# Leftover rows of four batches as seven half-size products, input loads issued behind GpSimd's first sums of the second chunk, both normalisations behind the second transpose

## The chip, the cores and the metric

The kernel runs on one core of a Trainium2 chip. The metric is the device time of one execution in microseconds (us). Three runs of the kernel before took 236.84, 237.04 and 237.11 us; their median, 237.04 us, is the time before. Engine names are those of the profile: PE is the matrix engine and PEld its weight load, DVE the vector engine, ACT the scalar engine, POOL is GpSimd, SP the sync engine, which here only issues DMAs.

## The reference, cut to what matters

There are 8 batches, each with 8 heads, 576 rows and 64 columns a head; `phi` gives 32 memory slots a head. An attention over the memory slots is followed by a gated feed-forward block with d_model 512 and d_ff 1536.

```python
a = exp(phi - max(phi, axis=2)); a = a / (sum(a, axis=2) + 1e-09)     # over the 576 rows
k_m = einsum('bhsm,bhsd->bhmd', a, k); v_m = einsum('bhsm,bhsd->bhmd', a, v)
scores = q @ k_m.T / 8; attn = softmax(scores)                         # over the 32 slots
x = (attn @ v_m), heads side by side                                   # 4608 x 512
out = (silu(x @ w_gate) * (x @ w_val)) @ w_out
```

## The kernel before, in words

**Stages of a batch.** The order of all instructions is written out by hand; each engine runs its own list in program order. For a batch the kernel exponentiates `phi` on ACT (`phi_exp`, line 176), forms the memory keys and values on PE (`kv_sum`, line 235) with their denominators (`kv_denominators`, line 263), scales them on DVE (`kv_reciprocal`, `kv_norm`, lines 267 and 271), and transposes them (`kv_T`). For batches 4 and on, `kv_T` is a DMA on SP's queue. The value side is folded into the weights (`u_round`, line 471, copied out of PSUM by ACT and DVE, lines 491 and 495). Scores (line 400) are exponentiated on ACT (line 411), their sums come from a transposing DVE reduction (`z_inv_v`, lines 434 to 443), and `norm` (line 451) gives the weights `t_A`.

**Gate and value slots.** 24 slots a batch (`gv_slot`) each make one gate and one value product (two matmuls each, line 514); ACT takes the gate through silu (line 531) and DVE multiplies it with the value (line 537) into `t_h`. A slot runs its gate, then the value and the multiplication of the slot before it. Eight slots make one of three chunks of d_ff.

**The output product.** `t_h` times `w_out` is done for the first 512 rows of a batch by a Winograd form: 7 products instead of 8 of half the size, each 12 matmuls of 128x256 (`products`, line 706). The left-hand sums `t_S` are made when a chunk is done (`chunk_done`, lines 601 and 559): on POOL for chunks 0 and 1, on DVE for chunk 2, four operations a chunk. PSUM banks are named `p_os`, `p_oa` and `p_oc`. ACT keeps three intermediate results (`keep`, line 729: `t_p` twice and `t_q`), DVE adds (line 734). In batches 0 to 6 the order is: first (two products, on s and then a), five (on c), six (on s, kept as `t_q`), three (on c), seven (on s again, over the same bank that `t_q` was copied from), four (on s).

**Leftover rows.** 64 rows of each batch remain. They are copied by POOL into `xs` (line 591), two batches side by side, and `out_rest` (line 654) multiplies them plainly: 12 matmuls a half, 24 a pair of batches, 96 in all.

**One iteration of the main loop, for batch b = 3 to 6.** It starts with product one of batch b-1 (6 units of 2 matmuls), then `loads(b)`, which has POOL issue four DMAs for batch b+2, in the order q, phi, k, v; then `scores(b)`, `u_values`, product two of batch b-1, `z_inv_v`, `norm`, product five, `phi_exp(b+1)` on ACT, `z_inv_v` and `norm` for the second half, product six, products three and seven. Then come the 24 slots. `spread` lays other work among them: what is left of batch b-1's units (product four, then 6 units of `out_rest`), after the eighth slot `kv_items(b+1)` with one `u_item` and two units behind it, and around slot 19 `u_three(b+1)`. `load_qT(b+1)`, a transposing DMA on SP's queue, and `phi_sum(b+1)`, six POOL operations (lines 215 to 224) that make the denominators a matter of two matmuls, stand at the head of the slots. For b = 2 `loads(2)` stands at slot 7 and batch 3 has no `phi_sum`. Iteration 7 has neither loads nor a next batch.

**Double buffers.** `phi` and `k`/`v` have two buffers each, q one for even and one for odd batches.

Of the kernel before, what the change touches and what calls it, by code (L numbers as in the profile page):

```python
# [14 lines left out]
def kernel(  # L15
# [19 lines left out]
    nc = tc.nc  # L35
# [173 lines left out]
    def phi_sum(b):  # L209
# [4 lines left out]
        mark = att.tile([1, 1], BF16, tag="mark", bufs=1, name="t_mark")  # L214
        nc.gpsimd.tensor_copy(out=mark, in_=atts[b - 1, 1][0:1, 0, 0:1])  # L215
# [81 lines left out]
    def kv_items(b, beside=None):  # L297


        def run_sums():  # L300
            o = 2 * D
            p = [bank([128, CH], FP32, f"p_kv{g}") for g in range(NG)]
            kv_denominators(b, p[0][:, o:o + NG])
            kv_sum(b, p, (0, 1))
            kv_reciprocal(b, p[0][:, o:o + NG])
            kv_norm(b, p)
            done(*p)
            if beside:
                beside()

        return [run_sums, lambda: kv_T(b)]
# [273 lines left out]
    def chunk_done(b, c):  # L585
# [21 lines left out]
        end = c + 1 == NCH  # L607
        if (b, c) in ((0, 2), (1, 1), (1, 2)):
            late.append(lambda *part: sums(nc.gpsimd if b else nc.vector, *part))
        else:  # L610
            sums(nc.vector if end else nc.gpsimd)
        if end and b > 1:
            late.append(ends)
        else:
            ends()
        if (b, c) in beside_sums:
            beside_sums[b, c]()

# [4 lines left out]
    }  # L623

# [10 lines left out]
    def store(t_o, b, t0, count, row=0, cols=slice(0, 512), queues=None):  # L635
# [3 lines left out]
        for n, (r0, m, bb, jj, pp) in enumerate(token_segments(b, t0, count)):  # L639
            eng = queues[n % len(queues)] if queues else nc.sync  # L640
            eng.dma_start(out=out_r[bb, jj, pp:pp + m, cols], in_=t_o[row + r0:row + r0 + m])

    def out_rest(pair, half):

        h = DM // 2
        mine = {}
        cols = slice(h * half, h * half + h)

        def unit(n):
            def run():  # L650
                if n == 0:
                    mine["p"] = bank([128, h], FP32, "p_oo")
                for jf in (2 * n, 2 * n + 1):
                    nc.tensor.matmul(  # L654
                        mine["p"],
                        lhsT=xs[pair][:, jf].rearrange("p a t -> p (a t)"),
                        rhs=WO[jf][:, cols],
                        start=(jf == 0),
                        stop=(jf == NJF - 1),
                    )  # L660
                if n == NJF // 2 - 1:
                    t_o = work.tile([128, h], FP32, tag="to", name="t_o")
                    copy("v" if box.get("end") else "a", t_o, mine["p"])
                    done(mine["p"])
                    end = 2 * pair + 2 == B
                    for k in range(2):
                        store(
                            t_o, 2 * pair + k, S - 64, 64, 64 * k, cols,
                            ((nc.sync, nc.scalar)[k],) if end else None,
                        )  # L670

            return run

        return [unit(n) for n in range(NJF // 2)]

    def products(b, by_hand):
# [3 lines left out]
        lo, hi = slice(0, h), slice(h, DM)  # L680

        def A(e, n):
            return lambda c, m, u: hts[b, c][
# [3 lines left out]
        def Sx(n):  # L687
            return lambda c, m, u: Ss[b, c][:, n, m, 128 * u:128 * u + 128]
# [7 lines left out]
        def product(home, lhs, rhs, after):  # L696
            def unit(k):
                c, m = k // 2, k % 2

                def run():  # L700
                    fresh = k == 0 and home not in mine
                    if fresh:
                        mine[home] = bank([128, 2, h], FP32, f"p_o{home}")
                        mine[home, "new"] = True
                    for u in range(2):
# [21 lines left out]
        def keep(name, home):  # L727
            def run():
                nc.scalar.copy(out=tile_of(name, tag=name, bufs=1), in_=mine[home])
# [8 lines left out]
        def both(name, t0, cols):  # L738
            for u in range(2):
                store(mine[name][:, u, cols], b, t0 + 128 * u, 128, cols=cols)  # L740

        def c11():
            t = tile_of("o1", (128, 2, DM), tag="to")
            add(t[:, :, lo], "a", "p1", True)
            if box.get("end"):
                both("o1", 0, lo)

        def c22():
            t = tile_of("o2", (128, 2, DM), tag="to")
            add(t[:, :, hi], "s", "p5")  # L750
            if box.get("end"):
                both("o2", 256, hi)

        def c12():
            t = mine["o1"]
            add(t[:, :, hi], "c", "q6", True)
            both("o1", 0, hi if box.get("end") else slice(0, DM))

        def c21():
            t = mine["o2"]  # L760
            copy("v" if box.get("end") else "a", t[:, :, lo], mine["s"])
            done(mine["s"])
            both("o2", 256, lo if box.get("end") else slice(0, DM))
# [4 lines left out]
        )  # L768
        now = {n: f for n, f in ops.items() if n not in by_hand}
# [6 lines left out]
        if b + 1 == B:  # L776
# [177 lines left out]
    for b in range(2, B):  # L954
        last = b + 1 == B
        exp_tables()
        if b == 2:
# [15 lines left out]
            mark = att.tile([1, 1], BF16, tag="mark", bufs=1, name="t_mark")  # L973
            nc.gpsimd.tensor_copy(out=mark, in_=Ts[2][0:1, 3, 0, 0:1])
# [5 lines left out]
        else:  # L980
            backlog += out_rest(b // 2 - 1, b % 2)
            run(take(6))
        if b > 2:
            loads(b)
# [9 lines left out]
        norm(b, 0)  # L994
# [4 lines left out]
        z_inv_v(b, 1)  # L999
        norm(b, 1)  # L1000
        run(take(6))
        run_late()
        nc.scalar.preload_act_table_set("silu_and_others")
        run(take(12))
        if b == 2:
            u_three(2)
            run(out_rest(0, 0))
            u_values(2)
            backlog = one[36:]
        g = gv_slots(b)  # L1010
        beside = 0 if last else min(7, len(backlog))
        outs = [lambda: run(take(1)) for _ in range(len(backlog) - beside)]
        streams = [(g, 0, 24), (outs, 4, 24)]
        if last:
            streams += [([u_item(b, 2)], 5, 6)]
        if not last:
            load_qT(b + 1)
            if b > 2:
                phi_sum(b + 1)
            else:  # L1020
                streams += [([lambda: loads(2)], 7, 8)]
            streams += [
                (kv_items(b + 1, lambda: (u_item(b, 2, "aava")(), run(take(2)))), KV, KV + 4),
                ([lambda: (run(take(2)), u_three(b + 1), run(take(3)))], 19, 20),
# [8 lines left out]
    run(out_rest(B // 2 - 1, 0))  # L1033
# [4 lines left out]
    run(out_rest(B // 2 - 1, 1))  # L1038
# [28 lines left out]
```

The softmax here doesn't subtract the row's maximum and nothing guards it: scores larger than these inputs give would overflow.

## Time and profile before

| what | value |
|---|---|
| median of three runs | 237.04 us |
| the profiled execution's own time | 236.3 us |
| its span, first to last instruction | 234.5 us |
| PE busy | 225.9 us, 96% |
| DVE, ACT, POOL busy | 187.4, 172.5, 135.2 us |
| last matmul ends | 230.2 us |
| POOL starts chunk 0's sums in batches 2 to 6 | 84.36, 109.25, 134.49, 159.79, 185.09 us |
| POOL issues the phi load of batches 4 to 7 | 74.80, 95.45, 119.86, 145.10 us |
| ACT starts `phi_exp` of batches 4 to 7 | 98.45, 124.08, 149.31, 174.62 us |

All times within the execution count from the start of the span. The profiled execution took 236.3 us, 0.74 us less than the median; its span leaves out 1.8 us around it. In the timeline view a row has the start, the time from the first start to the last end of the merged instructions, the engine, the line of the kernel, the operation, what it writes and reads, how many instructions the row merges and, in brackets, the idle time before it and what ended it. For matmuls such a row ends about 0.16 us after the next one has started, since they are pipelined.

### The profile page before, as it was taken

How to read it: one execution, taken by the hardware profiler on the slowest of the kernel's cores; microseconds unless marked ns; L12 is line 12 of the kernel's file. 1: busy time of each engine (PE TensorE's matmuls, PEld its weight loads, DVE VectorE, ACT ScalarE, POOL GpSimd, SP SyncE). 2: the span in 40 equal slices, each digit the busy share in tenths (PEclk: the TensorE clock that was granted, in tenths of full speed). 3: DMA queues.
4: the chain of work that ended last, by engine and by line, in shares of the span. 5: the costliest groups of instructions: out<-in, count | busy, mean ns of one | idle time of the engine just before them, and what ended most of it. 6: DMA issues, size and time to landing. Idle time of an engine off the chain costs nothing.

```text
span 234.5 us, 7300 instructions
## 1 busy us (share of the span) xinstructions
PE 225.9 (96%) x2847; PEld 171.3 (73%) x2847; DVE 187.4 (80%) x417; ACT 172.5 (74%) x368; POOL 135.2 (58%) x171
## 2 busy tenths in 40 slices
PE   7998899999999999999999999999999999999992
PEld 2555466778887777887778777877788777878881
DVE  4157699999979697998799878988799879987621
ACT  2758888988447888977898779968897789677310
POOL 8532426999099159654992399267916493029400
PEclk9999999999999999999999999999999999999999
DMA  6999999999974999899559964999313721122134
GB/s 211 205 205 207 198 208 206 228 238 248 207 169 97 252 216 158 166 247 232 137 80 252 214 110 106 225 226 142 110 25 81 132 89 27 31 62 89 33 92 126
DMA packets 42914, 36.84 MB, mean 157 GB/s; under 512 B 15488, under 2 KB 38528, under 8 KB 42880
## 3 DMA queue, kind: packets, MB, share of 16 engines
q0 software_dynamic: 21440, 22.42, 55.0%
q1 hardware_dynamic: 20176, 12.79, 25.8%
q10 hardware_dynamic: 1264, 1.18, 1.6%
q8 instruction: 22, 0.36, 0.6%
q14 instruction: 12, 0.10, 0.1%
HBM read 42.47 MB, written 9.44 MB: 221 GB/s over the span
## 4 chain that ended last, share of the span: by engine, by line
PE 82%; DMA 8%; POOL 4%; DVE 3%; issue 1%; ACT 0%; DVEq 0%; POOLq 0%
PE p_g L514 20%; PE p_v L514 19%; PE p_os L706 16%; PE p_oc L706 8%; DMA t_kv<-in_v_dram 8%; PE p_u L471 5%; PE p_oo L654 5%; PE p_oa L706 4%; PE p_kv L235 2%; POOL t_es L217 1%; POOL t_q L108 1%; PE p_g L400 1%; POOL t_kv L98 1%; DVE t_lz L443 1%; DVE t_z L434 1%
## 5 line engine op out<-in xcount | busy, mean ns | idle before, releaser
L537 DVE TENSOR_TENSOR t_h<-t_sg,p_v 128x288 bf16<-128x288 bf16 x192 | 83.1, 452 | 15.6 <-PE p_v L514 7.6
L514 PEld LDWEIGHTS <-t_U 128*128 128x128 bf16 x768 | 73.7, 98 | 21.7 <-issue 2.9
L531 ACT ACTIVATE t_sg<-p_g 128x288 bf16<-128x288 f32 x192 | 74.5, 423 | 15.9 <-PE p_g L514 9.1
L514 PE MATMUL p_g<-t_A,t_U 128*128 128x288 bf16 x384 | 77.2, 286 | 0.0
L514 PE MATMUL p_v<-t_A,t_U 128*128 128x288 bf16 x384 | 77.0, 286 | 0.0
L706 PEld LDWEIGHTS <-t_S 128*128 128x128 bf16 x384 | 37.4, 98 | 4.5 <-issue 0.2
L601 POOL TENSOR_TENSOR t_S<-t_h 128x512 bf16<-128x512 bf16 x17 | 19.7, 1156 | 35.2 <-DVE t_h L537 35.2
L491 ACT CAST t_U<-p_u 128x512 bf16<-128x512 f32 x53 | 28.0, 608 | 8.9 <-PE p_u L471 8.9
L706 PEld LDWEIGHTS <-t_h 128*128 128x128 bf16 x288 | 27.3, 98 | 7.8 <-issue 4.0
L706 PE MATMUL p_os<-t_T,t_S 128*128 128x256 bf16 x192 | 23.7, 273 | 0.0
L559 POOL TENSOR_TENSOR t_S<-t_S,t_h 128x512 bf16<-128x512 bf16 x17 | 19.6, 1155 | 1.3
L559 POOL TENSOR_TENSOR t_S<-t_h,t_S 128x512 bf16<-128x512 bf16 x17 | 20.1, 1186 | 0.0
L559 POOL TENSOR_TENSOR t_S<-t_h 128x512 bf16<-128x512 bf16 x17 | 19.6, 1155 | 0.0
L471 PE MATMUL p_u<-W,t_kT 64*32 64x512 bf16 (+1 forms) x416 | 15.9, 363 | 0.1
L706 PE MATMUL p_os<-t_T,t_h 128*128 128x256 bf16 x96 | 15.6, 273 | 0.0
L827 PE MATMUL p_warm<-bones 128*128 128x512 bf16 (+2 forms) x43 | 12.9, 427 | 1.7 <-DVE bones L850 1.7
L451 DVE TENSOR_TENSOR t_A<-t_E,t_lz 128x576 bf16<-128x576 bf16 x16 | 13.4, 840 | 0.9 <-ACT t_lz L427 0.3
L654 PE MATMUL p_oo<-WO,t_x 128*128 128x256 bf16 x96 | 14.0, 273 | 0.0
L495 DVE CAST t_U<-p_u 128x512 bf16<-128x512 f32 x19 | 12.4, 683 | 1.6 <-PE p_u L471 1.6
L215 POOL COPY t_mark<-t_A 1x1 bf16<-1x1 bf16 x4 | 0.7, 182 | 20.3 <-DVE t_A L451 20.3
L706 PE MATMUL p_oc<-t_T,t_S 128*128 128x256 bf16 x96 | 12.0, 273 | 0.0
L706 PE MATMUL p_oa<-WO,t_h 128*128 128x256 bf16 x96 | 11.8, 273 | 0.0
(93 smaller groups left out, 309.9 us busy)
## 6 DMA issues: line engine op xcount, KB each, us to landing
t_kv<-in_k_dram POOLq DMA_DIRECT2D x8, 576.0 KB, 10.1
t_kv<-in_v_dram POOLq DMA_DIRECT2D x8, 576.0 KB, 14.4
out_dram<-t_o SPq DMA_DIRECT2D x21, 192.0 KB, 2.6
t_phi<-in_phi_dram POOLq DMA_DIRECT2D x6, 576.0 KB, 7.9
t_q<-in_q_dram POOLq DMA_DIRECT2D x5, 576.0 KB, 7.4
out_dram<-t_o SPq DMA_DIRECT2D x37, 64.0 KB, 2.0
out_dram<-t_o SPq DMA_DIRECT2D x14, 128.0 KB, 5.8
t_q<-in_q_dram POOLq DMA_DIRECT2D x6, 288.0 KB, 11.3
```

What stands on the lines that cost most here:

```text
L451: nc.vector.tensor_tensor(out=a, in0=es.pop((b, g)), in1=lzs.pop((b, g)), op=ALU.mult)
L471: nc.tensor.matmul(p[g][32 * i:32 * i + 32, o:o + n], lhsT=kTs[b][64 * g:64 * g + 64, 2, 32 * i:32 * i + 32], rhs=w_part(w, c, i, g, halve ...
L491: nc.scalar.copy(out=t, in_=p)
L495: nc.vector.tensor_copy(out=t, in_=p)
L514: nc.tensor.matmul(p[:, 0:HALF], lhsT=Us[b, c, g][:, o // 2, which, 128 * (o % 2):128 * (o % 2 + 1)], rhs=atts[b, g][:, r], start=(g == 0) ...
L531: nc.scalar.activation(out=sg, in_=gate[:, 0:HALF], func=AF.Silu)
L537: nc.vector.tensor_tensor(out=dst, in0=sg, in1=val[:, 0:HALF], op=ALU.mult)
L559: eng.tensor_tensor(out=out, in0=x, in1=y, op=ALU.subtract)
L601: eng.tensor_tensor(out=t[:, 0], in0=A21, in1=A22, op=ALU.add)
L654: nc.tensor.matmul(mine["p"], lhsT=xs[pair][:, jf].rearrange("p a t -> p (a t)"), rhs=WO[jf][:, cols], start=(jf == 0), stop=(jf == NJF - 1),)
L706: nc.tensor.matmul(mine[home][:, u], lhsT=lhs(c, m, u), rhs=rhs(c, m), start=fresh and u == 0, stop=(k == 5), skip_group_check=u == 1 or n ...
L827: nc.tensor.matmul(p[:, 0:128 * a], lhsT=bones, rhs=x.to_broadcast([128, a, 128]) if a > 1 else bones, start=True, stop=True,)
```

## The change

Six things change.

1. The leftovers of four batches (two `xs` tiles of 128 rows) are one 256-row block, done as seven Winograd products of half the rows: 6 matmuls a product, 42 for four batches in place of 48. `out_rest` is gone. The left-hand sums come from `quad_sums`: 12 operations on 128x256 elements, on POOL for batches 0 to 3; for batches 4 to 7 nine on POOL and three on DVE. The first block stands in iteration 4, 12 units in slots 0 to 3 and 30 in slots 12 to 18.5; the second has 12 units in iteration 7's slots and 30 at the end.
2. `loads(b)`, for all b from 2, moves from the head of iteration b (slot 7 for b = 2) into `chunk_done(b, 1)`: POOL issues the four DMAs after the first two sums of chunk 1 and a copy.
3. From batch 2 on POOL's other two sums of chunk 1 come behind chunk 2's sums on DVE; POOL waits for these with a one-element copy (`wait_for`).
4. In `kv_items` of batches 4, 6 and 7 the denominators, and with them the reciprocal and the scaling on DVE, come behind the sums, the `u_item` and its two units. For batch 5 there is no `phi_sum`; its denominators are nine matmuls ahead of the sums, as for batch 3 before.
5. Both `norm` calls stand behind the second `z_inv_v`.
6. Product four of the batch before is spread thinner: 2 units in slots 3 to 24, two behind `u_item`, two behind `u_three`; in iteration 4 all six in slots 3 to 7. Stores alternate between queues at the end.

```diff
@@ phi_sum, new wait_for @@
-        mark = att.tile([1, 1], BF16, tag="mark", bufs=1, name="t_mark")
-        nc.gpsimd.tensor_copy(out=mark, in_=atts[b - 1, 1][0:1, 0, 0:1])
+        wait_for(atts[b - 1, 1][0:1, 0, 0:1])
...
+    def wait_for(x):
+        t = att.tile([1, 1], BF16, tag="mark", bufs=1, name="t_mark")
+        nc.gpsimd.tensor_copy(out=t, in_=x)
@@ kv_items @@
-            kv_denominators(b, p[0][:, o:o + NG])
+            behind = b in esums
+            if not behind:
+                kv_denominators(b, p[0][:, o:o + NG])
             kv_sum(b, p, (0, 1))
+            if behind:
+                beside()
+                kv_denominators(b, p[0][:, o:o + NG])
             kv_reciprocal(b, p[0][:, o:o + NG])
             kv_norm(b, p)
             done(*p)
-            if beside:
+            if beside and not behind:
                 beside()
@@ chunk_done @@
+        fourth = b in (3, 7)
         if (b, c) in ((0, 2), (1, 1), (1, 2)):
             late.append(lambda *part: sums(nc.gpsimd if b else nc.vector, *part))
+        elif b < 2:
+            sums(nc.gpsimd)
+        elif end:
+            sums(nc.vector)
+            wait_for(t[0:1, 3, 0, 0:1])
+            for part in ((2,), (3,)) if b + 1 == B else ((3,), (2,)):
+                for f in second:
+                    f(nc.gpsimd, part)
+            second.clear()
         else:
-            sums(nc.vector if end else nc.gpsimd)
-        if end and b > 1:
+            if c:
+                sums(nc.gpsimd, (0, 1))
+                second.append(sums)
+            else:
+                sums(nc.gpsimd)
+        if end and b > 1 and not fourth:
             late.append(ends)
         else:
             ends()
+        if b > 1 and c == 1:
+            loads(b)
+        if b + 1 == B and end:
+            quad_sums(1, (0, 1, 2))
@@ quad_sums, new @@
+        for n in parts:
+            for c in range(NCH):
+                t = Qs[qd, c]
+                A11, A12, A21, A22 = quarters(c)
+                if n == 0:
+                    nc.gpsimd.tensor_tensor(out=t[:, 0], in0=A21, in1=A22, op=ALU.add)
+                elif n == 1:
+                    subtract(nc.gpsimd, t[:, 1], t[:, 0], A11)
+                elif n == 2:
+                    subtract(nc.gpsimd, A21, A11, A21)
+                else:
+                    subtract(nc.vector if qd else nc.gpsimd, t[:, 2], A12, t[:, 1])
@@ products(b, by_hand, quad=None) @@
+        U = 2 if quad is None else 1
...
-                    for u in range(2):
+                    for u in range(U):
...
+        if quad is not None:
+            ops.update(
+                c11=leftover("c11", None, 0, lo), c12=leftover("c12", "q6", 1, hi),
+                c22=leftover("c22", "p5", 1, hi), c21=leftover("c21", "q6", 0, lo),
+            )
-        if b + 1 == B:
+        if quad is not None or b + 1 == B:
             return first + six + five + seven + three + four, ops
@@ main loop @@
         else:
-            backlog += out_rest(b // 2 - 1, b % 2)
             run(take(6))
-        if b > 2:
-            loads(b)
...
         z_inv_v(b, 0)
-        norm(b, 0)
         ops["c11"]()
         run(take(6))
         if not last:
             phi_exp(b + 1)
         z_inv_v(b, 1)
+        norm(b, 0)
         norm(b, 1)
         run(take(6))
         run_late()
+        if b == 4:
+            wait_for(atts[4, 1][0:1, 0, 0:1])
+            quad_sums(0)
...
         if b == 2:
             u_three(2)
-            run(out_rest(0, 0))
+            run(one[36:])
             u_values(2)
-            backlog = one[36:]
         g = gv_slots(b)
-        beside = 0 if last else min(7, len(backlog))
+        quad = []
+        if b == 4:
+            quad = products(b, (), 0)[0]
+        if last:
+            rest, rest_ops = products(b, (), 1)
+            backlog += rest[:12]
+        beside = 0 if last or quad else min(4, len(backlog))
         outs = [lambda: run(take(1)) for _ in range(len(backlog) - beside)]
-        streams = [(g, 0, 24), (outs, 4, 24)]
+        streams = [(g, 0, 24), (quad[:12], 0, 3), (quad[12:], 12, 18.5)]
+        streams += [(outs, 3, 7 if quad else 24)]
...
-            if b > 2:
+            if b > 2 and b != 4:
                 phi_sum(b + 1)
-            else:
-                streams += [([lambda: loads(2)], 7, 8)]
             streams += [
                 (kv_items(b + 1, lambda: (u_item(b, 2, "aava")(), run(take(2)))), KV, KV + 4),
-                ([lambda: (run(take(2)), u_three(b + 1), run(take(3)))], 19, 20),
+                ([lambda: (u_three(b + 1), run(take(2)))], 19, 20),
             ]
...
     ops["p1"]()
-    run(out_rest(B // 2 - 1, 0))
     box["end"] = True
     run(take(6))
     ops["c11"]()
     run(backlog)
-    run(out_rest(B // 2 - 1, 1))
+    quad_sums(1, (3,))
+    run(rest[12:])
```

## The prediction

> **What bounds the kernel now.** I read the page first: busy shares, then the chain that ended last.
>
> ```profile
> PE 225.9 (96%) x2847; PEld 171.3 (73%) x2847; DVE 187.4 (80%) x417; ACT 172.5 (74%) x368; POOL 135.2 (58%) x171
> PE 82%; DMA 8%; POOL 4%; DVE 3%; issue 1%; ACT 0%; DVEq 0%; POOLq 0%
> ```
>
> PE is the bound. The view of waits names only two for PE itself, 1.7 and 0.8 us, both before 26 us. A change pays if it takes matmuls from PE and makes nothing late; whatever comes late costs in full. So next I read the timeline of POOL, in batch 3 and at the start of iteration 4.
>
> ```profile
> 109.25 1.15 POOL L601 TENSOR_TENSOR t_S<-t_h 128x512 bf16<-128x512 bf16 x1 [3.25 <-DVE t_h L537]
> ...
> 114.16 1.15 POOL L601 TENSOR_TENSOR t_S<-t_h 128x512 bf16<-128x512 bf16 x1
> 115.39 1.16 POOL L559 TENSOR_TENSOR t_S<-t_S,t_h 128x512 bf16<-128x512 bf16 x1
> 116.51 1.15 POOL L559 TENSOR_TENSOR t_S<-t_h 128x512 bf16<-128x512 bf16 x1
> ...
> 118.71 0.41 POOL L591 COPY t_x<-t_h 128x256 bf16<-128x256 bf16 x1
> 119.05 0.81 POOL L115 DMA_DIRECT2D t_q<-in_q_dram  x1
> 119.86 0.80 POOL L93 DMA_DIRECT2D t_phi<-in_phi_dram  x1
> ```
>
> 109.25 is the start of chunk 0's sums; I call it S(3). 114.16 begins chunk 1. The phi load at 119.86 is batch 6's and is used an iteration later. Its landing, from the view of DMA issues by window (columns: name, count, KB, us to landing):
>
> ```profile
> t_q<-in_q_dram POOLq DMA_DIRECT2D x1, 576.0 KB, 6.6
> t_phi<-in_phi_dram POOLq DMA_DIRECT2D x1, 576.0 KB, 7.2
> ```
>
> The other three such phi loads took 7.7, 7.9 and 7.9 us, the q loads ahead of them 6.4 to 7.4. Last, ACT and PE where phi is used, in iteration 4:
>
> ```profile
> 123.59 0.59 ACT L729 COPY t_p<-p_oc 128x512 f32<-128x512 f32 x1 [0.26 <-PE p_oc L706]
> 124.08 1.17 ACT L176 ACTIVATE t_ephi<-t_phi 128x1152 bf16<-128x1152 f32 x1
> 125.14 0.58 ACT L729 COPY t_q<-p_os 128x512 f32<-128x512 f32 x1
> ```
>
> ```profile
> 124.70 1.47 PE L706 MATMUL p_oc<-WO,t_S 128*128 128x256 bf16 x12
> 126.01 1.47 PE L706 MATMUL p_os<-t_T,t_S 128*128 128x256 bf16 x12
> 127.32 0.65 PE L514 MATMUL p_g<-t_A,t_U 128*128 128x288 bf16 x4
> ```
>
> ACT works in order: the copy t_q stands behind the exponential of the next batch's phi. PE's product seven (126.01) overwrites the bank that t_q copies, so it waits for that copy. Today the copy ends at 125.72, 0.3 us ahead, and phi has been there for 20 us.
>
> **The change, part by part.**
>
> *Matmuls.* 12 matmuls of 128x256 go at 1.31/12 = 0.109 us (126.01 to 127.32): -1.31. Batch 5's denominators are nine matmuls (0.30 us, 80.97 to 81.27) for two (0.19): +0.11. The denominators' waits for POOL go in batches 4, 6, 7 (0.40, 0.26, 0.25 us from their row to the sums' row, about 0.1 of it work): -0.5. Together -1.7 on PE.
>
> *Loads.* Formerly loads(3) was issued at 94.64; now it comes in iteration 3 after chunk 1's first two sums. From S to phi's issue: 114.16-109.25 = 4.91, two sums 116.51-114.16 = 2.35, copy 0.34, q's issue 0.81; 8.41 us. Landing: rows say 7.2 to 7.9; q's shortest 6.4, plus 1.35 (phi behind q in three loads), less 0.81, would give 6.9. I take 7.5. So phi is there at S+15.9. When is it wanted? In before product seven starts at 126.01-109.25 = S+16.76. Between lie 16 matmuls of leftovers and product four; six are left, so PE would come at 16.76-1.74+0.65 = S+15.67. But phi gives seven only at 15.91 + 1.06 (exponential) + 0.58 (copy) + 0.1 (hand-over, an estimate from 132.21 to 132.25 and the like) = S+17.65. PE stands for 2.0 us in a plain iteration.
>
> The Trainium skill ("DMA: Bandwidth & Descriptors", section "Anatomy of one DMA") gives a fit of 2.0 us plus bytes over 436 GB/s. By it q and phi together, 1.18 MB, would take 4.7 us, phi would be in time and the case would be the first rival. The rows of this kernel show 7.2 and more, and the rows decide.
>
> *Denominators behind.* PE: priced above. DVE: the reciprocal and four scalings (132.25 to 133.45) now follow u_item's cast and two units (0.44 us), and the multiplication that ends chunk 0 stands behind them: S comes 0.5 us later after the sums (bounds 0 and 0.6), 3.6 instead of 134.49-131.41 = 3.08. The transposing DMA of that result waited 1.8 us behind SP's other transpose anyway (ready 133.45, issued 135.26): nothing. If that cover went, u_three (4.9 us after the issue, whose landing took 4.2) would wait. Six banks are taken at once by sums and u_item: 0 to 0.3, I take 0, since casts free one each 0.5 us.
>
> *POOL's queue.* Behind the four issues (3.1 us) stand a mark and two sums of chunk 1. Loads end at S+10.7; chunk 2's DVE sums end at 121.30, S+12.05: covered. Mark and two sums, 0.2 and 2.3 us, end at S+14.6; product three (124.70, S+15.45) wants the first of them after its first four matmuls: 0. The mark's wait costs nothing more, POOL has only a copy and phi's sums behind it. SP: q lands at S+15.0, its transpose was issued at 129.87, S+20.6: 0.
>
> *Quad sums.* On POOL about 0.67 us each (between 1.16 for 512 and 0.43 for 128 columns): 12 take 8 us in iteration 4, from about 127.2 to 135.5; S(4) is 139: covered by 4 us. At the end, nine take 6 us after chunk 2's DVE sums, mark, two sums and copy (together 5.4 us behind the last slot); the third set would be up to 0.6 us late for product seven: I take 0.3.
>
> *Both norms behind.* The first gate needs both; DVE's total is equal; 0. Thinner spreading: PE comes 0.4 us earlier out of the slots than DVE and ACT (which gains a 0.6 us copy there), and t_A was ready only 0.14 us ahead of the gate (127.18, 127.32). So gates may wait 0 to 0.6; hidden where PE stands for phi, 0.5 in iteration 7.
>
> **The sum, from S to S.** Seven to the next sums: 1.31, eight gates and seven values 3.68 (131.22-127.32 less one unit 0.22), 0.15 change of tile shape: 5.14. A plain loop: 8.41+7.5+1.74+5.14+3.6 = 26.4 us.
>
> - Iteration 3: 26.4 against 109.25-84.36 = 24.9: +1.5.
> - Iteration 4 has 24 more matmuls ahead of the sums (2.62), nine denominators (0.11), no delay of 0.5: 28.6 against 25.24: +3.4.
> - Iteration 5: 30 matmuls of the first block lie after S(4), and no units beside u_item (-0.44): PE at 16.76-1.74+3.27-0.44 = S+17.85, phi at 17.65: no stall. 17.85+5.14+3.6 = 26.6 against 25.3: +1.3.
> - Iteration 6: 26.4 against 25.3: +1.1.
>
> That makes S(6) +7.3. From there to the end: S is 0.5 late on DVE but not on PE (-0.5), 54 leftover and product-four matmuls after batch 7's sums for 58 (-0.44), gates +0.5, quad sums +0.3: about -0.1. Sum +7.1. On the profiled execution's own time: 236.3+7.1 = 243.4 us. The runs' median lay 0.74 above that execution; the same on top gives **244.1 us**.
>
> PE's stalls of some 2 us might cost clock. In these rows the granted clock stays 1.00 in every stretch I asked for, but no idle time of PE over 1.7 us is among them. The skill ("TensorE: Matmul & The Clock Gate", "What's actually happening") says that the clock halves after an idle window of about 3.4 us; by that a 2 us stall costs none, one of 3.4 would make the next microseconds twice as long.
>
> **The rivals.**
>
> 1. *Faster: phi is in time.* If phi landed within 15.67-1.74-8.41 = 5.5 us of its issue, seven would not wait and -1.7 stands: 235.3 us. For it: the loads now run with less other traffic, and DVE's sums no longer run beside their start. Against: four rows of 7.2 to 7.9, and even with the shortest q 6.9. Chance 7%.
> 2. *Same: phi in time, DVE's chain ends last.* Then gates wait for t_A 0.5 us in three iterations: -1.7+1.5, 236.8 us. For: the 0.14 us margin. Against: the same rows. 5%.
> 3. *Slower still: v is late too.* PE reaches the sums at S+22.8 (8.41+7.5+1.74+5.14); v is issued 1.53 after phi, at S+9.94, and took 13.0 to 13.7: S+22.9 to 23.7. If so 0.9 us more in three iterations: 246.8 us. Against: v's last packets were slowed by stores and transposes that now fall later. 13%.
>
> The forecast itself, 75%: low end with landing 6.9 (-0.6 in three loops) and no 0.5 on DVE (-1.5): 240.8; high end with 7.9 and v: about 247.5. Range **240.5 to 247.5**; it leaves out rivals 1 and 2 and a little beside. A run of this kernel can tell about 0.2% from no change: faster 0.07, same 0.05, slower 0.88.
>
> **What would show it.** In the profile after: ACT's exponential of phi idle until a DMA of t_phi, about 2 us in iterations 3, 4 and 6 and near nothing in 5; PE waiting for ACT's t_q at product seven; S(b) 26 to 27 us apart, 28 to 29 from 3 to 4; PE with 2842 matmuls; no wait for POOL at the denominators; the phi issue 8.4 us after S. I am wrong if phi lands in under 6 us, if S to phi's issue is shorter, or if PE's gaps sit elsewhere.

## The result, and the profile after

The changed kernel takes 248.85 us, the median of four runs (248.25, 248.36, 249.34, 251.91); the kernel before, run beside it, 236.94. The ratio is 1.0528, 95% interval 1.044 to 1.0616: slower, as forecast, but above the range of 240.5 to 247.5. The profiled execution took 248.36 us, with a span of 246.6. Executions of one kernel differ in how often the clock of PE drops, and the intervals leave out the runs that this lengthens most, the medians do not.

The page of the changed kernel, busy line, granted clock by slice and chain:

```profile
PE 227.8 (92%) x2842; PEld 171.2 (69%) x2842; DVE 187.8 (76%) x426; ACT 173.4 (70%) x368; POOL 144.9 (59%) x192
...
PEclk9999999999999999999997999999999999999999
...
PE 53%; DMA 20%; POOL 13%; DVE 7%; ACT 2%; issue 2%; ACTq 0%; DVEq 0%; POOLq 0%
```

PE did five matmuls less and was busy 1.9 us longer. Of the chain, 82% was PE before; now PE has 53% and DMA and POOL a third. One slice of the clock reads 7. The view of waits (us in total, times, longest) says where:

```profile
ACT t_ephi L176 <- DMA t_phi<-in_phi_dram: 10.2, 4, 3.6
...
PE p_os L740 <- ACT t_q L765: 9.8, 5, 3.3
```

Neither line was there before. ACT waits in four iterations for phi, PE in the same four for the copy that stands behind phi's exponential (its fifth wait, 0.9 us, is in the tail). The timeline of ACT, then of PE, at that place in iteration 4:

```profile
127.71 1.16 ACT L176 ACTIVATE t_ephi<-t_phi 128x1152 bf16<-128x1152 f32 x1 [3.62 <-DMA t_phi<-in_phi_dram]
128.78 0.57 ACT L765 COPY t_q<-p_os 128x512 f32<-128x512 f32 x1
```

```profile
129.40 2.69 PE L740 MATMUL p_os<-t_T,t_S 128*128 128x256 bf16 x12 [3.31 <-ACT t_q L765]
```

Phi landed at 127.69; exponential, copy and product seven follow without a gap. The same twelve matmuls took 1.47 us before and take 2.69 here. The view by windows (start:end, length, busy time of each engine, then granted clock and DMA) gives the reason:

```profile
126.00:130.00 4.00, 0.69 (x5) 0.43 (x4) 1.73 (x3) 2.27 (x3) 2.76 (x6) 0.93 1.18 219
130.00:134.00 4.00, 4.00 (x25) 2.92 (x24) 0.76 (x2) 1.59 (x4) 4.00 (x7) 0.64 1.10 255
```

PE stood still from 126 on, and the clock was granted at half from 129.5 to 132.9 us by the trace's clock records: 3.41 us at half speed, some 1.7 us lost.

### The profile page after: what moved, and what is told of

It reads as the page before. It is cut to its first block, busy times and chain, and to the rows that moved or that the text cites. A ratio compares the mean times of both kernels' runs of the same rounds, so it can differ in the third digit from the quotient of the medians.

```text
span 246.6 us, 7325 instructions
## 1 busy us (share of the span) xinstructions
PE 227.8 (92%) x2842; PEld 171.2 (69%) x2842; DVE 187.8 (76%) x426; ACT 173.4 (70%) x368; POOL 144.9 (59%) x192
## 4 chain that ended last, share of the span: by engine, by line
PE 53%; DMA 20%; POOL 13%; DVE 7%; ACT 2%; issue 2%; ACTq 0%; DVEq 0%; POOLq 0%
PE p_g L518 14%; PE p_v L518 14%; DMA t_phi<-in_phi_dram 13%; PE p_os L740 13%; DMA t_kv<-in_v_dram 7%; POOL t_S L563 6%; PE p_oc L740 4%; POOL t_S L605 3%; PE p_u L475 3%; PE p_oa L740 2%; PE p_kv L234 2%; DVE t_bkv L270 1%; ACT t_ephi L176 1%; POOL t_q L115 1%; POOL t_x L595 1%
## 5 line engine op out<-in xcount | busy, mean ns | idle before, releaser
L541 DVE TENSOR_TENSOR t_h<-t_sg,p_v 128x288 bf16<-128x288 bf16 x192 | 81.8, 452 | 19.1 <-PE p_v L518 7.5
L740 PEld LDWEIGHTS <-t_S 128*128 128x128 bf16 x384 | 37.9, 99 | 14.7 <-issue 9.9
L740 PE MATMUL p_os<-t_T,t_S 128*128 128x256 bf16 x192 | 24.9, 281 | 8.9 <-ACT t_q L765 8.9
L563 POOL TENSOR_TENSOR t_S<-t_h,t_S 128x512 bf16<-128x512 bf16 x17 | 19.5, 1150 | 0.0
L740 PE MATMUL p_os<-t_T,t_h 128*128 128x256 bf16 x96 | 14.5, 273 | 0.3 <-DVE t_o L770 0.3
L176 ACT ACTIVATE t_ephi<-t_phi 128x1152 bf16<-128x1152 f32 x6 | 7.0, 1164 | 10.2 <-DMA t_phi<-in_phi_dram 10.2
L455 DVE TENSOR_TENSOR t_A<-t_E,t_lz 128x576 bf16<-128x576 bf16 x16 | 12.8, 831 | 0.3 <-ACT t_lz L431 0.3
L770 DVE TENSOR_TENSOR t_o<-p_os,t_p 128x512 f32<-128x512 f32 x8 | 5.5, 688 | 8.4 <-PE p_os L740 5.1
```

The costliest lines, as they stand in the source:

```text
L176: nc.scalar.activation(out=t.rearrange("p j i m -> p i j m"), in_=phis.pop(b).rearrange("p i (j m) -> p i j m", m=M), func=AF.Exp,)
L455: nc.vector.tensor_tensor(out=a, in0=es.pop((b, g)), in1=lzs.pop((b, g)), op=ALU.mult)
L541: nc.vector.tensor_tensor(out=dst, in0=sg, in1=val[:, 0:HALF], op=ALU.mult)
L563: eng.tensor_tensor(out=out, in0=x, in1=y, op=ALU.subtract)
L740: nc.tensor.matmul(mine[home][:, u], lhsT=lhs(c, m, u), rhs=rhs(c, m), start=fresh and u == 0, stop=(k == 5), skip_group_check=u == 1 or n ...
```

## The experiments

Ratios are to the kernel before, run on the same chip. "S" is, as in the prediction, the start of chunk 0's sums on POOL.

### 1. The loads alone, and put back at the head

*e1: changed kernel, loads at the head of the iteration again.*

```diff
-        if b > 1 and c == 1:
-            loads(b)
...
+        if b > 2:
+            loads(b)
...
+        if b == 2:
+            streams += [([lambda: loads(2)], 7, 8)]
```

> The changed kernel with one part undone: the loads for batch b+2 stand again at the head of iteration b (batch 4's between slots 7 and 8 of iteration 2), as in the kernel before; all else stays changed. Theory (the late loads are the whole loss: phi comes late, product seven waits for the copy t_q behind its exponential, one wait of over 3 us halves the clock): the four waits of 1.3 to 3.5 us (9.7 in sum) and the half clock (about 1.6) go, 235 to 237.5 us, and no wait for t_phi on ACT. Rival (the half-size products, the denominators behind and the norms behind cost the time themselves): 243 us or more.

253.31 us, ratio 1.0646 (1.0598 to 1.0695): slower still. The expected 235 to 237.5 fell. PE waits for phi nowhere, but 11.1 us for the transposed k (longest 5.5). POOL's timeline shows that the loads are not where they were:

```profile
95.51 0.18 POOL L644 COPY t_mark<-t_S 1x1 bf16<-1x1 bf16 x1 [2.93 <-DVE t_S L563]
95.65 1.14 POOL L563 TENSOR_TENSOR t_S<-t_h,t_S 128x512 bf16<-128x512 bf16 x1
96.76 1.15 POOL L563 TENSOR_TENSOR t_S<-t_h 128x512 bf16<-128x512 bf16 x1
97.86 0.81 POOL L115 DMA_DIRECT2D t_q<-in_q_dram  x1
98.66 0.79 POOL L93 DMA_DIRECT2D t_phi<-in_phi_dram  x1
```

At the head they stand behind part 3 of the change, the mark and chunk 1's second half: phi goes out at 98.66, not at 95.45. So this does not undo the move of the loads; parts 2 and 3 belong together.

*e2: kernel before, loads behind the first two sums of chunk 1, nothing else.*

```diff
+        elif b > 1 and c == 1:
+            sums(nc.gpsimd, (0, 1))
+            ends()
+            loads(b)
+            sums(nc.gpsimd, (2, 3))
+            return
...
-        if b > 2:
-            loads(b)
...
-            else:
-                streams += [([lambda: loads(2)], 7, 8)]
```

> The kernel before with that one part alone: the loads for batch b+2 behind the first two sums of batch b's chunk 1 on POOL, nothing else. Theory: phi is late here too, but PE reaches product seven 1.1 us later than in the changed kernel (ten more leftover matmuls ahead of it), so the four waits come to 5 to 7 us and none is long enough for the clock: 241 to 245 us. Rival (the other parts cost most of it): 237 to 239 us.

246.54 us, 1.0391 (1.0331 to 1.045). PE waits 6.5 us for ACT's t_q at product seven in four places (longest 3.5), as in the changed kernel. Late loads alone cost about three quarters of it (3.9% of 5.3%), and more than I expected: phi's first landing took 9.6 us, with four stores issued within 1.2 us of it, the clock was at half once, and gates waited 1.3 us for DVE's t_A.

### 2. Late loads, and what makes PE wait for them

*e3: changed kernel, phi issued ahead of q. e4: changed kernel, `phi_exp` moved behind product three. e10: changed kernel, order phi, k, v, q.*

```diff
@@ e3 @@
-            load_q(b + 2)
             load_phi(b + 2, nc.gpsimd)
+            load_q(b + 2)
@@ e4 @@
-        if not last:
-            phi_exp(b + 1)
         z_inv_v(b, 1)
...
-        run(take(12))
+        run(take(6))
+        if not last:
+            phi_exp(b + 1)
...
+        run(take(6))
@@ e10 @@
-            load_q(b + 2)
             load_phi(b + 2, nc.gpsimd)
             load_k(b + 2)
             load_v(b + 2)
+            load_q(b + 2)
```

> The changed kernel with phi's load issued ahead of q's, nothing else. Theory: phi is issued 0.8 us sooner and lands in the 6 to 7 us that the first load of the four has taken so far, so it is there about 2 us sooner; the waits at product seven shrink to 0 to 1.5 us, the half clock goes: 239 to 242 us. If the landing is set by all the traffic and not by the place in the queue: phi gains only 0.8 us, 244 to 246 us. If phi is not the cause: 248 us or more.

> The changed kernel with the exponential of the next batch's phi placed behind product three instead of ahead of product six, loads as late as before: the copy t_q no longer stands behind it. Theory (PE waits only because of the order on ACT): PE goes straight into product seven, and the wait turns up smaller at the gates, whose silu now stands behind the exponential: 238 to 242 us. Rival (ACT cannot catch up, the whole wait moves to the gates): 246 us or more.

> The changed kernel with the loads as late as it has them, in the order phi, k, v, q (q is wanted last). With phi alone put first, phi came in 5 to 6 us and PE then waited for v (3.0, 1.5, 3.8 us). Theory (the loads' lateness is the whole loss, spread over phi and v): v comes 2 to 3 us sooner, PE's waits shrink to 0 to 1 us each, no half clock: 239 to 243 us. If q's transpose then comes late and u or scores wait for it: 244 to 248 us.

e3 took 249.28 us, 1.0505 (1.0438 to 1.0573); e4 248.68, 1.0479 (1.0414 to 1.0544): no gain that these intervals can tell, against expectations of 238 to 242. In e3 phi lands in 5.0 to 6.0 us, and the waits of PE read:

```profile
PE p_kv L234 <- DMA t_kv<-in_v_dram: 7.6, 3, 3.6
PE p_warm L890 <- DVE bones L913: 1.7, 1, 1.7
PE p_os L740 <- ACT t_q L765: 1.4, 2, 0.9
```

The wait at product seven is gone (the 1.4 us left are in the tail), and PE now waits at the sums for v, which in the changed kernel had landed 0.1 and 0.5 us ahead of PE's sums in iterations 3 and 6. e4 shows the same: outside the tail no wait at product seven, 5.8 us for v and 1.2 us at the gates. So it was ACT's order that had passed phi's lateness on to product seven. Rival 3, v late too, was thus not wrong as a mechanism; it stood right behind phi. e10 serves both: 240.43 us, 1.0153 (1.0118 to 1.0187), 8.4 us less than the changed kernel, from the order of the four load calls alone. Phi lands in 4.4 to 6.0 us, v in 9.5 to 11.5 (12.0 to 12.9 in the changed kernel), q, last, in 12.3 to 14.8. No wait for phi or v is left, and a smaller one has come up:

```profile
PE p_u L475 <- DMA t_kT<-t_bkv: 2.7, 2, 1.4
PE p_os L740 <- ACT t_q L765: 1.8, 2, 0.9
```

### 3. Why the waits were longer than forecast

*e12: changed kernel, the four stores of a batch's second half moved behind those of the next batch's first half. e13: the 30 later half-size matmuls of batches 0 to 3 in slots 17 to 24. e14: both.*

```diff
@@ e12 @@
-            both("o2", 256, lo if end else slice(0, DM))
+            if 1 < b < 6:
+                held_stores.append(lambda: both("o2", 256, slice(0, DM)))
+            else:
+                both("o2", 256, lo if end else slice(0, DM))
...
             both("o1", 0, hi if end else slice(0, DM))
+            run(held_stores)
+            held_stores.clear()
@@ e13 @@
-        streams = [(g, 0, 24), (quad[:12], 0, 3), (quad[12:], 12, 18.5)]
+        streams = [(g, 0, 24), (quad[:12], 0, 3), (quad[12:], 17, 24)]
```

> The changed kernel with one thing moved: the four stores of the second half of a batch's output, which SP issues within 1 us of the loads of q and phi at 118 and 178 us, go behind the four stores of the first half of the next batch (batches 2 to 5). Theory A (phi took 8.8 and 8.2 us there, not the 6.8 of iteration 3, because these stores share the DMA engines with it): phi lands in 6.5 to 7.2 us in iterations 4 and 6, the waits at product seven shrink by 2.0 and 1.4 us, and with the first of them below 3 us the half clock (1.6 us) goes: 243 to 245.5 us. Theory B (the landing varies for another reason): 248 to 249.5 us.

> The changed kernel with the 30 later half-size matmuls of batches 0 to 3 in slots 17 to 24 of iteration 4 instead of 12 to 18.5, so most of them come behind chunk 1. Theory A (the loads of iteration 4 went out 9.6 us after the start of chunk 0's sums instead of 8.4, because these matmuls held up chunk 1): the loads go out some 8.4 us after it again, phi is in time in iteration 5, its 1.3 us wait goes: 246.5 to 248 us. Theory B (the wait in iteration 5 comes from the landing alone): 248.3 to 249.5 us.

> Both of these edits. If the terms that the forecast had too small are the landing beside stores, the half clock behind it and the loads held up in iteration 4, this kernel has the time that was forecast for the changed one: 241.5 to 244.5 us. If not: 246 us or more.

The changed kernel's view of DMA issues between 117.9 and 119.6 us (KB each, median us to landing):

```profile
t_q<-in_q_dram POOLq DMA_DIRECT2D x1, 576.0 KB, 8.3
t_phi<-in_phi_dram POOLq DMA_DIRECT2D x1, 576.0 KB, 8.8
out_dram<-t_o SPq DMA_DIRECT2D x2, 192.0 KB, 5.4
out_dram<-t_o SPq DMA_DIRECT2D x2, 64.0 KB, 4.5
```

And e12's at the same place, 119.5 to 120.6 us, where no store is issued:

```profile
t_q<-in_q_dram POOLq DMA_DIRECT2D x1, 576.0 KB, 6.5
t_phi<-in_phi_dram POOLq DMA_DIRECT2D x1, 576.0 KB, 7.1
```

e12 took 245.22 us, 1.0368 (1.0332 to 1.0404): 3.6 us under the changed kernel. Phi lands in 7.10 and 7.05 us in iterations 4 and 6, for 8.82 and 8.17, and PE's idle time at product seven there shrinks from 3.3 and 2.7 to 1.6 and 1.5 us. Theory A holds in these two iterations: the stores beside the loads had made phi later. In iteration 5 e12 changes nothing: six stores of 64 KB of the half-size products go out in the 4 us ahead of phi's issue, in both kernels, and phi takes 8.33 us for 8.18.

e13 took 250.32 us, 1.054 (1.0493 to 1.0588): no gain. e14 took 245.7, 1.04 (1.0354 to 1.0446), the same as e12 within the intervals and between the two ranges that were expected. The mechanism is there in e14: in iteration 4 phi goes out 8.4 us after S, not 9.6; it takes 7.07 us, with the six small stores now 0.7 to 4.2 us behind it; and in iteration 5 ACT does not wait for it. But from S(4) to S(5) e14 needs 28.4 us and e12 too, since the matmuls now stand ahead of product seven itself. So these matmuls explain the late issue, and moving them gains nothing. e14's run at a mean clock of 1.00 took 244.82 us: without the stores ahead of the loads and without half clock the kernel has about the time that was forecast, 244.1. In part that is luck: e14's four loops take 25.6, 28.0, 28.4 and 25.5 us where 26.4, 28.6, 26.6 and 26.4 were forecast.

### 4. What the rest of the change is worth

*e5: changed kernel, loads at the changed place in POOL's order but one batch ahead. e6: e5 with the last batch's stores two to SP's queue for one to ACT's. e9: loads at the head, and chunk 1's four sums on POOL in one piece, so that no mark stands ahead of them (batch 4's as in e5's last two lines). e11: e9 with e6's stores. e7: e5 with denominators and norms in the old order.*

```diff
@@ e5 @@
         if b > 1 and c == 1:
-            loads(b)
+            loads(b + 1)
...
+        if b == 2:
+            streams += [([lambda: loads(2)], 7, 8)]
@@ e6, in both() @@
+                    queues=(nc.sync, nc.sync, nc.scalar) if end else None,
@@ e9 @@
-            wait_for(t[0:1, 3, 0, 0:1])
-            for part in ((2,), (3,)) if b + 1 == B else ((3,), (2,)):
-                for f in second:
-                    f(nc.gpsimd, part)
-            second.clear()
...
-                sums(nc.gpsimd, (0, 1))
-                second.append(sums)
+            sums(nc.gpsimd)
...
-        if b > 1 and c == 1:
-            loads(b)
...
+        if b > 2:
+            loads(b)
@@ e7, on e5: kv_items and norms as in the kernel before @@
-            behind = b in esums
...
+        norm(b, 0)
         ops["c11"]()
...
-        norm(b, 0)
```

> The changed kernel with the loads at the changed place in POOL's order (behind the first two sums of chunk 1), but each set one batch sooner (batch b+3's behind batch b's sums; batch 4's between slots 7 and 8 of iteration 2): so they stand ahead of the mark that held them up in the run with the loads at the head. Theory (the time of the loads is the whole loss; the first run that put them back failed only because POOL's new mark stands ahead of them): no wait for t_phi or for v, no half clock, 235 to 237.5 us. Rival (the half-size products, or the order of denominators and norms, cost time themselves): 240 us or more.

> The same, and at the end the stores of batch 7's own tiles go two to SP's queue for one to ACT's. The 0.9 us wait for the copy t_q in the last product seven then shrinks if ACT's six store issues ahead of it (3.49 us) are what made it late: 0.3 to 0.6 us less than the kernel with the loads a batch ahead. If the last stores then come late on SP's queue: the same or up to 1 us more.

> The changed kernel with its half-size products, its denominators and its norms, but chunk 1's four sums on POOL in one piece again (no mark for chunk 2 and no second half behind it), and the loads at the head of the iteration: POOL's order around the loads is that of the kernel before. Theory (what is lost comes from when the loads are issued, also in the two runs that put them back incompletely): the loads start where they did, no wait for phi, v or the transposes of q and k, only the tail's 0.9 us stays: 235 to 237 us. Rival (the half-size products crowd POOL or the gates, whatever the loads do): 239 us or more.

> The kernel with whole sums and the loads at the head, and at the end the stores of batch 7's own tiles two to SP's queue for one to ACT's: 0.3 to 0.7 us under the one without that (it gave 0.5 where the loads were a batch ahead), so 234.5 to 236.5 us; it would be the version that beats both.

> The kernel with the loads a batch ahead, and with the denominators and the norms in the order of the kernel before: of the change only the half-size products are left. Theory: 12 matmuls less on PE (1.3 us) and 0.5 us more in the tail, so 0.5 to 1.5 us under the kernel before. Rival (the half-size products cost time through POOL's quad sums or the split sums): 238 us or more.

| kernel | us | ratio, 95% interval |
|---|---|---|
| e5 loads a batch ahead | 241.10 | 1.0198 (1.0158 to 1.0238) |
| e6 the same, other stores | 240.57 | 1.0170 (1.013 to 1.021) |
| e9 whole sums, loads at the head | 240.07 | 1.0152 (1.0118 to 1.0186) |
| e11 the same, other stores | 240.33 | 1.0153 (1.0125 to 1.0182) |
| e7 e5 with the old norms and denominators | 245.68 | 1.0383 (1.0349 to 1.0416) |

With the loads on time the changed kernel still loses 1.5 to 2%. My theory that their lateness is the whole loss falls. The waits of PE in e9:

```profile
PE p_os L729 <- ACT t_q L754: 1.5, 2, 0.9
PE p_u L475 <- DMA t_kT<-t_bkv: 1.4, 1, 1.4
PE p_g L404 <- DMA t_qT<-t_q: 1.3, 1, 1.3
```

The kernel before has none of the three. The two transposes are waited for in iteration 3, the transposed q for scores and the transposed k, at its end, for `u_three`. PE's rows there, in the kernel before and then in e9:

```profile
94.55 0.29 PE L400 MATMUL p_g<-t_qT,t_kT 64*32 64x288 bf16 x1
...
114.91 0.84 PE L471 MATMUL p_u<-W,t_kT 64*32 64x512 bf16 x24
```

```profile
95.41 0.29 PE L404 MATMUL p_g<-t_qT,t_kT 64*32 64x288 bf16 x1 [1.33 <-DMA t_qT<-t_q]
...
115.88 0.84 PE L475 MATMUL p_u<-W,t_kT 64*32 64x512 bf16 x24 [1.39 <-DMA t_kT<-t_bkv]
```

In the kernel before the transposes landed at 94.06 and 114.40, and PE came 0.5 us behind each. In e9 they land at 95.37 and 115.83, and PE would come at 94.1 and 114.5. Two things make the waits. From scores to `u_three` PE needs 1.3 us less: four leftover matmuls and four of product four fewer stand there (0.9 us), and the wait at the denominators (0.4 us) is gone. They had been cover. But the transposed q of the first wait is itself 1.3 us later, as is v before it (landed at 93.98 for 92.77), and PE comes only 0.5 us sooner; why v is later was not tested. So what was taken from iterations 2 and 3 is given back as waits. The 30 matmuls more in iteration 4 cost in full (scores of iteration 4 to 5: 29.2 us for 25.2), and iterations 5 and 6 keep their gain (24.0 us each for 25.3). In the tail the copies t_q come late twice (0.6 and 0.9 us of PE). In e11 and e9 the last one starts 0.1 us after ACT's last store issue ends (231.83 and 232.15 us), with four issues as with six; that store waits for DVE's last copy (231.18 us in e9). In e6 PE waits 1.1 and 0.8 us for these copies, in e5 0.7 and 0.9. Fewer stores on ACT's queue thus gave nothing that these runs can tell; whether the issue or something else sets the tail stays open.

e7 is 4.6 us slower than e5. Its profile has two waits of PE that e5's has not:

```profile
PE p_g L513 <- DVE t_A L450: 2.3, 3, 0.8
...
PE p_kv L262 <- POOL t_ehl L223: 0.8, 3, 0.3
```

Gates wait for DVE's t_A, denominators for POOL, and 3.4 us go by at half clock (1.7 us lost); together that is 4.8 of the 5.4 us by which this profile is longer than e5's. The half clock is not the main part: one of e7's runs at a mean clock of 1.00 took 245.41 us too. So the new order of denominators and norms, which is worth 0.3% in the kernel before, is what keeps the gates in time here; e7 undoes both at once and does not tell which of them does.

*e8, e18: kernel before with denominators behind and norms behind. e16, e17: norms alone, denominators alone. e15: e8 with the order phi, k, v, q.* The edits in the kernel before (e15 adds e10's):

```diff
@@ e17, and with e16's e8 and e18: kv_items as in the change @@
+            behind = b in esums
+            if not behind:
+                kv_denominators(b, p[0][:, o:o + NG])
...
+            if behind:
+                beside()
+                kv_denominators(b, p[0][:, o:o + NG])
@@ e16: main loop @@
-        norm(b, 0)
         ops["c11"]()
...
         z_inv_v(b, 1)
+        norm(b, 0)
         norm(b, 1)
```

> The kernel before with two parts alone: the denominators behind the sums where phi's sum is on POOL, and both norms behind the second transpose. Theory: the denominators' waits (0.5 us) go, the rest is covered: 236.3 to 237.2 us. Rival (S comes 0.5 us later in each loop, or gates wait for t_A): 238 to 240 us.

> The kernel before with the denominators behind and both norms behind (0.3% under the kernel before when made alone), and its loads, at their old place, in the order phi, k, v, q. In the run without the new order u waited 1.4 and 0.6 us for the transposed k, which waits for v. Theory: v comes 3 us sooner, both waits go: 234 to 235.5 us, the version that beats both kernels. Rival: q comes later and its transpose holds up SP, nothing is won: 236 us or more.

> The kernel before with both norms behind the second transpose and nothing else. The forecast had this at 0: PE and DVE do the same work, the first gate needs both. Then within 0.2% of the kernel before, 236.2 to 237.0 us.

> The kernel before with the denominators behind the sums and nothing else. The forecast had 0.5 us of waits for POOL gone on PE, and chunk 0's sums 0.5 us later on DVE, under cover: 235.9 to 236.6 us. If u then waits for the transposed k (1.4 and 0.6 us in the run of both edits), the gain goes there: 236.5 to 238 us.

> Both edits on the kernel before, a second time. The first time gave 0.3% less than the kernel before, with an interval that left out no change by 0.1%. If that was real: 235.5 to 236.5 us and a ratio below 1 again; if it was chance: within 0.2%.

All but e15 came out as expected. e8 took 236.32 us, ratio 0.9968 (0.9945 to 0.999); repeated as e18 235.87, 0.9968 (0.9945 to 0.999). e17 took 235.93, 0.9969 (0.9946 to 0.9993), e16 236.43, 0.9993 (0.9968 to 1.0019). So the denominators alone give 0.3%, some 0.7 us, and the norms nothing that these runs can tell. e17 is the version that beats both kernels, if by little. e15 took 236.75, 1.0007 (0.9989 to 1.0025): v lands 4.5 to 5.6 us sooner than in e8, but u's waits for the transposed k stay (1.8 us in all for 1.3), so v was not their cause; the rival held. In both profiles the transposed k lands 0.3 to 1.3 us behind the transposed q, and in e15 q is the load that lands last.

## Why the prediction was wrong

The sign and the mechanism were right: phi comes late, ACT's order passes it on to product seven, PE stands. The size was not. The terms of the loop, forecast and as the profile after has them (us; differences of starts and landings; "it" is the iteration):

| term | forecast | it 3 | it 4 | it 5 | it 6 |
|---|---|---|---|---|---|
| S to phi's issue | 8.41 | 8.39 | 8.39 | 9.57 | 8.38 |
| phi's landing | 7.5 | 6.76 | 8.82 | 8.18 | 8.17 |
| landing to product seven | 1.74 | 1.71 | 1.71 | 1.77 | 1.71 |
| seven to the next sums | 5.14; it 4 7.87 | 5.16 | 9.56 | 5.08 | 5.07 |
| sums to S | 3.6; it 4 3.1 | 3.50 | 3.09 | 3.51 | 3.51 |
| S to S | 26.4, 28.6, 26.6, 26.4 | 25.5 | 31.6 | 28.1 | 26.8 |

The four loops are 4.0 us longer than forecast. S(2) is 0.6 us later than in the kernel before (0.3 of it already at the sums at 59 us, ahead of all that was changed), and the tail from S(6) is 0.2 us longer where it was to be 0.1 shorter. Together that makes the 248.36 of the profiled execution against the forecast 243.4. Of the 4.0 us in the loops, the landing makes 1.9, the half clock 1.7 and the late issue in one iteration 1.2; small terms the other way make up the rest.

**Matmuls, POOL's queue, ACT's and PE's order.** Right: four of the five terms are within 0.2 us, but for two cells. One reading was short: the full view names two more waits of PE in the kernel before, 0.5 and 0.2 us, also before 30 us, and nothing hangs on them. POOL's quad sums were covered (127.4 to 134.9 us), the denominators' waits are gone, and PE did 2842 matmuls.

**Landing, 7.5 us.** This step failed. The four rows it came from had been taken as a property of the load. But stores had been in flight beside each of the four. In the changed kernel loads are issued when other stores are: landings are 6.76 with no store in flight, 8.17 to 8.82 with stores issued up to 4 us ahead or beside; e12 took those of iterations 4 and 6 away and had 7.10 and 7.05. In all profiles, phi as the second load took 6.8 to 7.1 us with no store in flight, and 6.9 to 9.6 with some, so which stores matter is only in part shown. I moved the loads past queues of instructions, and did not look which transfers of SP's queue would run beside them. It gave 1.3, 0.7 and 0.7 us too little in iterations 4 to 6, and 0.7 too much in iteration 3.

**"A 2 us stall costs none" of the clock.** This failed too, once by its premise and once by itself; the sum had put the clock at nothing. The stall in iteration 4 was 3.3 us, not 2, and the next 3.41 us ran at half clock: seven to the sums took 9.56 for 7.87, 1.7 us (in e12 and e14, at full clock there, the same stretch takes 7.90). And in e12's profile a stall of 2.1 us in iteration 3 has a window at half clock behind it. I had no such stall to look at, since the kernel before has none, and went by the Trainium skill ("TensorE: Matmul & The Clock Gate", "What's actually happening"), which has the clock drop after an idle window of about 3.4 us. The runs here differ: 2.1 us idle, three fifths of a window, were enough in e12, and they decide.

**Iteration 5 without a stall.** Wrong: phi's issue came 1.2 us late, since the 30 half-size matmuls lie ahead of chunk 1's end. I had counted them for PE's arrival at product seven, and not for the end of chunk 1 that lets the loads go. e14 had 8.4 us with them later.

**Gates, quad sums and tail.** Gates waited in no iteration (forecast 0.5 in iteration 7). In the tail the last product seven waited 0.9 us, not for quad sums (forecast 0.3) but for the copy t_q.

**Rivals.** Rival 1, 235.3 us if phi is in time, is refuted as a whole: with phi in time the kernel takes 240.1 (e9), 240.4 (e10) or 249 (e3). Behind phi stood v, and behind v the transposes and the tail. Rival 2's wait for t_A did not come; it does with the old order of norms and denominators and the loads late (e2, 1.3 us) or a batch ahead (e7, 2.3 us). Rival 3's v landed 0.1 us ahead of the sums in iteration 3 and 0.5 us in iteration 6, so it cost nothing in the changed kernel; it did as soon as PE no longer stood for phi (e3, e4).

**The gain of 1.7 us on PE** was real for the denominators (0.7 us in e17, forecast 0.5). The 12 matmuls saved bring nothing in the total of any version tried: e9 gains 1.3 us in each of iterations 5 and 6, and pays for it in iteration 4, in waits for the transposes and in the tail.

## What to carry to other kernels

Before a load is moved later, list all that waits for its set (here phi, v, the transposes of q and k) with each one's margin: curing the first only shows the next, and the order inside the set can be worth as much as the place (here 8.4 us in e10, and 8.8 in e9, which also puts chunk 1's sums back). Price its landing by what is issued on the other queues in the microseconds around it, not by its rows at the old place. Matmuls that look like waste may be the cover of a transfer; ask what PE would reach sooner without them.

## What the hardware showed that was not expected

**The clock drops by windows on a fixed grid.** In all profiles the stretches at half clock, but for the last one at the end of the trace, are 3.41 us long or twice that, and in e4 two of them begin 81.92 us apart, 24 times 3.413. Laying that grid over PE's idle time in all 20 profiles (the time between matmuls, whose ends the profile models) gives: eleven grid windows at full clock had 1.96 us of idle time or more (57%), and all were followed by one at half; of all the others, with 1.83 us or less, none was. So 2.1 us inside one window cost a half window (e12), and 2.7 us that lay over two, 1.1 and 1.6 us, cost none (e3). With the clock already at half, 0.7 us (e1) and 1.2 us (e13) of idle time were followed by a second window at half, 0.4 us (e13) and less were not. The Trainium skill's section named above gives the same free-running window of 3413 ns. The view by windows of e12:

```profile
98.00:102.00 4.00, 1.91 (x18) 1.57 (x17) 2.81 (x6) 1.75 (x3) 0.90 (x3) 1.00 1.15 255
102.00:106.00 4.00, 4.00 (x23) 2.77 (x23) 1.74 (x3) 2.40 (x4) 2.94 (x6) 0.63 1.18 252
```

PE is idle for 2.1 us of the first window, and the second is granted at 0.63. Where the grid lies differs from run to run, so a stall near 2 us can cost a half window in one run and none in the next. That fits the scatter of such kernels: e14's six runs had mean clocks from 0.989 to 1.000 and took 244.5 to 247.6 us.

**Place in the queue.** Over all profiles phi's load took 4.4 to 6.0 us as the first of the four (e3, e10, e15), 6.8 to 9.6 as the second, with the same bytes.

**A transposing DMA beside loads.** The transpose of q took 4.9 to 7.6 us where the last load landed before its issue or at most 3 us after it, and 7.3 to 15.3 us where that load had 4.5 us or more to go; it then landed 0.9 to 4.8 us after the load (kernel before: issued 129.87, v landed 134.41, transpose 139.15; e1: 134.81, 146.52, 149.94).
